# Attention and a low-rank mixed feed-forward block on one core: each raw weight block loaded as two transfers of half a row

## The chip, the cores and the metric

The kernel runs on one core of a Trainium2 chip. A core has four engines that compute (TensorE for matrix products, VectorE, ScalarE, GpSimd), SyncE, which here only issues transfers, and 16 DMA engines that move data between device memory (HBM) and on-chip memory. Each engine works through its own list of instructions in order; semaphores hold an instruction until what it needs is there. In the profile the engines are PE, DVE, ACT, POOL and SP. The metric is the device time of one execution in microseconds (us). One more execution of each kernel is recorded by the hardware profiler, and the rows below come from that one.

## The reference

The inputs are q, k and v (4 batches, 12 heads, 448 positions, 64 per head), two rank-32 matrices U and V, and two weight matrices w_ch1 (768 x 3072) and w_ch2 (3072 x 768). The scale is 1/8, the cap is 30.

```python
scores = scale * np.matmul(q, k.transpose(0, 1, 3, 2))
scores = cap * np.tanh(scores / cap)
scores = scores - np.max(scores, axis=-1, keepdims=True)
attn = np.exp(scores)
attn = attn / (np.sum(attn, axis=-1, keepdims=True) + 1e-09)
x = np.matmul(attn, v)              # heads put side by side: x is (4, 448, 768)
xt = x.transpose(0, 2, 1)
h = xt @ U @ V                      # mixing along the sequence
u = x + h.transpose(0, 2, 1)
ch = np.maximum(u @ w_ch1, 0.0) @ w_ch2
out = u + ch
```

The weights reach the kernel as raw words of 64 bits, so a block of 128 x 768 numbers is 128 rows of 6,144 bytes. The kernel turns them into 32-bit numbers itself.

## The kernel before

**Stages.** The program has three parts, which overlap at their edges. Up to about 225 us it is attention (scores, tanh, exp, product with v, the division by the sums, the mixing with U and V). From about 197 to 538 us comes the first pass of the feed-forward block, over batches 0 and 1; from 538 us on the second pass, over batches 2 and 3. A pass goes through the 24 blocks of 128 hidden columns in 12 chunks of two blocks. Products are kept at 32-bit accuracy by splitting each operand into a high and a low part, so one product is three matmuls.

**Up and down.** `up_seven` (matmuls of line 851) forms relu(u @ w_ch1) of one chunk by seven products of combined operands in place of eight plain ones. `down` (line 916) multiplies the result of one chunk by its two blocks of w_ch2, twelve products of six matmuls, and adds them to `u`. In the first pass the products of `down` for one chunk are laid between the products of `up_seven` for the next. The `down` of the last chunk has no next chunk in its pass: its 72 matmuls stand in one piece between the last product of the first pass and the first product of the second. In the second pass `down_seven` (line 1049) takes the place of `down`.

**Weights.** In the first pass `block` fetches a raw block into a buffer `wr` (two of them), `convert` makes 32-bit numbers of it in `wa`, and `keep` writes them to HBM, from where the second pass reads them. `convert` is three tasks: ScalarE takes the upper words (line 335), VectorE shifts the lower words (line 340), VectorE joins both (line 343). For w_ch2 `weights` then splits the block into its high part (ScalarE, line 284) and its low part (VectorE, line 754) in a buffer `w1`, which `down` multiplies by. The first of `down`'s six matmuls of a product use the chunk's first block, the other three its second block, so the second block of the last chunk, block 23 of w_ch2, is wanted from the fourth matmul of that `down` on.

**Operands of the second pass.** `operands` and `part` make the seven `x` buffers of a pass out of `u`: sums of two parts of `u` (VectorE, line 691, in a buffer that is also named `wr`), the high part (ScalarE or VectorE, lines 284 and 286) and the low part (VectorE, line 698). An `x` buffer of the second pass comes free when the first pass has done with it.

**What sets the order.** The order on every engine is fixed before the program runs. Each piece of work is a task with an assumed duration on the engines that can do it, a latency after which others may use its result, a priority (a lower number goes first) and the buffers that it needs. `simulate` runs through the tasks on a clock of its own: whenever an engine is free, it takes the ready task with the lowest priority number. The order that comes out is emitted. `rank` shifts the priorities between -150 and 0 by the table RANK. The chunks 10 and 11 of the first pass are prepared with -60, the operands of the second pass with -50; RANK adds 108 to the conversion, 56 to the operands and 6 to the splitting of w_ch2. So in the two last chunks a conversion has priority 48, an operand of the second pass 6, the splitting of w_ch2 -54, and the sums into `u` and the relu -200. A load is a task on SP with an assumed duration (350 for one transfer) and latency.

Of the kernel before, what the change touches and what calls it, by code (L numbers as in the profile page):

```python
# [14 lines left out]
I32 = mybir.dt.int32  # L15
# [4 lines left out]
DM = H * D  # L20
# [270 lines left out]
class Build(Plan):  # L291
# [417 lines left out]
    def block(self, which, f, first, begin, prio):  # L709

        nc = self.nc
        a = self.buf("wa", [128, DM], F32, self.wp, self.late)
        if not first:
            self.task({"SP": 350}, lambda: nc.sync.dma_start(out=a.t, in_=self.kept[which, f]),
                r=[("kept", which, f)], w=[(a, 0)], lat=4000, prio=prio)
            return a
        raw = self.buf("wr", [128, 2 * DM], I32, self.wq)

        def load():
            nc.sync.dma_start(out=raw.t, in_=self.w[which][f].bitcast(I32))  # L720

        def keep():
            d = self.kept[which, f] = self.dp.tile([128, DM], F32, tag="kept", name="kept", bufs=2 * NF)
            nc.scalar.dma_start(out=d, in_=a.t)

        self.task({"SP": 350}, load, w=[(raw, "u"), (raw, "l")], lat=7500, prio=prio, begin=begin)
        self.convert(raw, lambda: raw.t, a, lambda: a.t, prio, DM)
        self.task({"ACT": 120}, keep, r=[(a, 0)], w=[("kept", which, f)], lat=6500, prio=prio)
        return a
# [292 lines left out]
    def down_seven(self, order, bs, m, gq, vs):  # L1022
# [4 lines left out]
        u0, u1 = (self.u_bufs[b] for b in bs)  # L1027
        block = lambda u, d: ((lambda: u.t[:, d]), (u, d))
        onto = {3: lambda d: block(u1, d), 1: lambda d: block(u0, d), 6: lambda d: block(u0, 3 + d), 5: lambda d: block(vs, d),
            2: lambda d: block(u0, d), 7: lambda d: block(u1, 3 + d), 4: lambda d: block(u0, 3 + d)}  # L1030
        if final:
            at = range(order, order + 21)
# [4 lines left out]
        for n, (p, d) in enumerate((p, d) for p in porder for d in range(3)):  # L1037
            fresh = p not in (6, 5, 4)
            if fresh:
                bank[d] = self.bank()  # L1040
            ps = bank[d]

            def products(ps=ps, p=p, d=d, fresh=fresh):
                sl = slice(128 * d, 128 * d + 128)
                w, g = wo[p].t, [x.t for x in go[p]]
                n = 0
                for k in range(2):
                    for wi, gi in ((0, 0), (0, 1), (1, 0)):
                        nc.tensor.matmul(  # L1049
                            ps.t[:, :S], w[:, wi, k, sl], g[gi][:, k], start=fresh and n == 0, stop=n == 5,  # L1050
                            skip_group_check=not fresh)
                        n += 1

            self.task({"PE": 6 * 206}, products, r=[*((wo[p], i, k) for i in range(2) for k in range(2)), *((x, 0) for x in go[p])], w=[(ps, 0)],
                prio=next(at), mode="mm")
            out, key = onto[p](d)
            if p == 5 and m == 0:
                self.task({"ACT": 560}, lambda ps=ps, out=out: self.copy(nc.scalar, out(), ps.t[:, :S]), r=[(ps, 0)], w=[key],
                    prio=-200)
            elif p == 5 and final:  # L1060
                for x in (d, 3 + d):
                    self.onto(ps, *block(u1, x), False)
            else:
                self.onto(ps, out, key, n % 2 if not final else n < 15)
            yield
# [97 lines left out]
```

## Time and profile before

| what | value |
|---|---|
| median of 3 runs | 855.48 us (855.27 to 856.4) |
| profiled execution, its own time | 853.6 us |
| its span, first to last instruction | 851.8 us |
| matmuls busy (PE) | 840.4 us, 99% of the span |
| VectorE busy (DVE) | 691.0 us, 81% |
| ScalarE busy (ACT) | 527.6 us, 62% |
| moved by DMA | 136.51 MB, mean 160 GB/s |

The profiled execution's own time is 1.8 us more than its span. Busy time counts instructions that compute; issuing a transfer is not counted. A row of a waiting list says who waited for whom. A row of a timeline is one instruction, or several alike with their count (x3); in square brackets stands how long the engine was idle before it and what ended that.

### The profile page before, as it was taken

The page shows a single profiled execution, that of the slowest core. Times are in us where ns is not written, and L with a number is a line of the kernel's source. Part 1 is how long each engine was busy: PE and PEld are TensorE (multiplying, and loading weights), DVE is VectorE, ACT ScalarE, POOL GpSimd, SP SyncE. Part 2 cuts the span into 40 slices and gives each one's busy share as a digit, 9 for nine tenths or more (in the row PEclk, how much of TensorE's full clock was granted, in tenths as well). Part 3 has the DMA queues.
Part 4 walks back from the last instruction along what each step waited for, and adds up shares of the span by engine and source line. Part 5 has one row for each costly group of instructions (what it writes and reads, how often), then busy time and mean ns, then how long its engine had stood idle before and what let it go on. Part 6 is the DMA issues. An engine that isn't in the chain of part 4 may idle for free. (4 is left out here: it accounts for less than half of the span.)

```text
span 851.8 us, 11737 instructions
## 1 busy us (share of the span) xinstructions
PE 840.4 (99%) x4264; PEld 671.4 (79%) x4264; DVE 691.0 (81%) x1144; ACT 527.6 (62%) x789; POOL 146.1 (17%) x188
## 2 busy tenths in 40 slices
PE   9999999998999999999999999999999999999998
PEld 5334334346899999999999899999999999999997
DVE  2799889999887777877778699789888788888786
ACT  7999899885555355545555465456655555656472
POOL 0111111111022122122122122102111111111142
PEclk9999999999999999999999999999999999999999
DMA  6752443423578878787877866714427354262479
GB/s 225 241 172 84 160 148 96 146 68 93 183 190 259 245 188 249 191 265 211 231 231 207 252 162 151 215 48 120 114 36 179 68 143 93 53 170 42 122 136 224
DMA packets 51354, 136.51 MB, mean 160 GB/s; under 512 B 6720, under 2 KB 27104, under 8 KB 51296
## 3 DMA queue, kind: packets, MB, share of 16 engines
q1 hardware_dynamic: 23024, 79.29, 28.3%
q0 software_dynamic: 21360, 37.59, 24.6%
q10 hardware_dynamic: 6912, 18.88, 5.7%
q8 instruction: 33, 0.54, 0.3%
q14 instruction: 25, 0.20, 0.1%
HBM read 79.28 MB, written 24.47 MB: 122 GB/s over the span
## 5 line engine op out<-in xcount | busy, mean ns | idle before, releaser
L851 PE MATMUL mm<-x,ws 128*128 128x448 f32 x1512 | 332.7, 367 | 1.4 <-ACT cx L284 0.8
L851 PEld LDWEIGHTS mm<-x,ws 128*128 128x128 f32 x1512 | 283.3, 188 | 27.3 <-ACT cx L284 1.2
L916 PE MATMUL mm<-g,w 128*128 128x448 f32 x864 | 187.0, 366 | 0.6 <-DVE cx L864 0.3
L916 PEld LDWEIGHTS mm<-g,w 128*128 128x128 f32 x864 | 162.0, 188 | 15.0 <-ACT st L284 0.9
L1049 PE MATMUL mm<-g,w 128*128 128x448 f32 x696 | 154.9, 366 | 0.0
L284 ACT ACTIVATE st<-mm 128x448 f32<-128x448 f32 x133 | 72.4, 544 | 113.7 <-PE mm L916 55.2
L1049 PEld LDWEIGHTS mm<-g,w 128*128 128x128 f32 x696 | 130.6, 188 | 11.8
L929 POOL DMA_DIRECT2D u<-st x72 | 62.5, 868 | 268.9 <-ACT st L284 263.8
L1084 POOL DMA_DIRECT2D u<-st x57 | 49.4, 866 | 224.1 <-ACT st L284 161.4
L498 ACT ACTIVATE th<-sc,qsc 128x896 f32<-128x896 f32 x84 | 80.3, 1005 | 11.9 <-PE sc L493 11.7
L493 PE MATMUL sc<-qk 64*128 64x448 f32 (+1 forms) x384 | 77.8, 573 | 0.0
L508 ACT ACTIVATE th<-th,capt 128x1792 f32<-128x1792 f32 x42 | 75.2, 1790 | 0.8
L921 DVE TENSOR_TENSOR u<-u,mm 128x448 f32<-128x448 f32 x72 | 44.5, 618 | 21.6 <-PE mm L916 19.9
L534 PE MATMUL o<-th,vn 128*64 128x448 f32 x288 | 59.4, 548 | 0.0
L493 PEld LDWEIGHTS sc<-qk 64*128 64x128 f32 (+1 forms) x384 | 27.2, 175 | 37.2 <-issue 18.9
L343 DVE SCALAR_TENSOR_TENSOR wa<-wa,wr 128x768 int32<-128x768 int32 (+2 forms) x50 | 46.7, 935 | 11.1 <-ACT wa L335 10.3
L698 DVE TENSOR_TENSOR ws<-ta,ws 128x384 fp32r<-128x384 f32 x96 | 53.0, 552 | 3.2 <-ACT ws L284 2.9
L1079 DVE TENSOR_TENSOR u<-u,mm 128x448 f32<-128x448 f32 x57 | 35.0, 619 | 23.3 <-PE mm L1049 21.7
L540 DVE TENSOR_TENSOR es<-es,th 128x896 f32<-128x896 f32 (+1 forms) x44 | 47.5, 1082 | 6.0 <-ACT th L508 5.5
L335 ACT ACTIVATE wa<-wr 128x768 f32<-128x768 f32 (+2 forms) x50 | 44.1, 884 | 3.8 <-DVE wr L340 2.4
L534 PEld LDWEIGHTS o<-th,vn 128*64 128x64 f32 x288 | 18.5, 136 | 32.8 <-issue 30.0
L284 ACT ACTIVATE ws<-ta 128x384 fp32r<-128x384 f32 x64 | 32.9, 519 | 15.2 <-PE mm L851 8.9
(118 smaller groups left out, 957.5 us busy)
## 6 DMA issues: line engine op xcount, KB each, us to landing
wr<-in_w SPq DMA_DIRECT2D x48, 768.0 KB, 5.7
u<-st POOLq DMA_DIRECT2D x129, 224.0 KB, 4.1
kept<-wa ACTq DMA_DIRECT2D x48, 384.0 KB, 5.8
qk<-in_qk SPq DMA_DIRECT2D x24, 448.0 KB, 4.0
wr<-kept SPq DMA_DIRECT2D x24, 384.0 KB, 3.7
wa<-kept SPq DMA_DIRECT2D x24, 384.0 KB, 4.0
vn<-in_v SPq DMA_DIRECT2D x12, 448.0 KB, 3.7
rb<-rd POOLq DMA_DIRECT2D x24, 224.0 KB, 3.7
```

What stands on the lines that cost most here:

```text
L284: e.activation(out=out, in_=in_, func=func)
L493: nc.tensor.matmul(ps.t[out, a, :S], qks[c].t[hd, 1, 128 * t:min(S, 128 * t + 128)], qks[c].t[hd, 0], start=True, stop=True)
L498: nc.scalar.activation(out=th.t[:, j], in_=ps.t[:, :, :S], func=AF.Tanh, scale=self.qsc)
L508: nc.scalar.activation(out=th.t, in_=th.t, func=AF.Exp, scale=self.capt)
L534: nc.tensor.matmul(o.t[64 * a:64 * a + 64, :S], vn.t[:, 3 * i + t, a], th.t[:, j, a], start=False, stop=t == 2)
L540: e.tensor_tensor(out=out(), in0=in0(), in1=in1(), op=ALU.add)
L698: e.tensor_tensor(out=lo, in0=src(), in1=hi.bitcast(F32), op=ALU.subtract)
L851: nc.tensor.matmul(ps.t[:, :S], ws[p].t[:, wi, sl], xs[p].t[:, xi, d], start=fresh and n == 0, stop=n == 8, skip_group_check=not fresh)
L916: nc.tensor.matmul(ps.t[:, :S], w1[f].t[:, wi, sl], g[b, f].t[:, gi], start=f == fs[0] and i == 0, stop=f == fs[-1] and i == 2)
L929: nc.gpsimd.dma_start(out=u.t[:, d], in_=st.t, accum_op=ALU.add)
L1049: nc.tensor.matmul(ps.t[:, :S], w[:, wi, k, sl], g[gi][:, k], start=fresh and n == 0, stop=n == 5, skip_group_check=not fresh)
L1084: self.task({"POOL": 1000}, lambda: nc.gpsimd.dma_start(out=out(), in_=st.t, accum_op=ALU.add), r=[(st, 0)], w=[key], lat=6000, prio=-200)
```

## The change

The load of a raw block becomes two transfers, one for columns 0 to 767 and one for columns 768 to 1535 of its 1,536 words of 32 bits. Both go out on SP, one behind the other. The task's assumed duration on SP goes from 350 to 700 and its latency from 7500 to 7200.

```diff
         def load():
-            nc.sync.dma_start(out=raw.t, in_=self.w[which][f].bitcast(I32))
+            for i in range(2):
+                part = slice(DM * i, DM * i + DM)
+                nc.sync.dma_start(out=raw.t[:, part], in_=self.w[which][f].bitcast(I32)[:, part])
...
-        self.task({"SP": 350}, load, w=[(raw, "u"), (raw, "l")], lat=7500, prio=prio, begin=begin)
+        self.task({"SP": 700}, load, w=[(raw, "u"), (raw, "l")], lat=7200, prio=prio, begin=begin)
```

Since `simulate` reads both numbers, the order changes too. TensorE and GpSimd keep the order of their instructions from the first to the last. On VectorE and ScalarE the order is the same through attention and differs from the first pass on. Three places are shown. In the changed kernel, lines from 720 on have moved by up to 2, and the numbers behind the names differ between the two programs.

First place, VectorE in the last chunk of the first pass. Before, `wr_4344` is the raw block 23 of w_ch2 and `wa_4441` its converted form; `wr_4326` and `wa_4416` are block 22.

```order
L691 TENSOR_TENSOR ta_4346<-wa_4313,ta_4346 128x384
L340 TENSOR_SCALAR wr_4326<-wr_4326 128x768
L340 TENSOR_SCALAR wr_4344<-wr_4344 128x768
L864 TENSOR_TENSOR cx_4388<-cx_4388,mm_4240 128x448
L698 TENSOR_TENSOR ws_4427<-wa_4313,ws_4427 128x384
L921 TENSOR_TENSOR u1_558<-u1_558,mm_4420 128x448
L819 SCALAR_TENSOR_TENSOR g_4431<-cx_4388,g_4431 128x448
L343 SCALAR_TENSOR_TENSOR wa_4416<-wa_4416,wr_4326 128x768
L343 SCALAR_TENSOR_TENSOR wa_4441<-wa_4441,wr_4344 128x768
```

In the changed kernel block 22 is `wr_4405` and `wa_4518`, and block 23 is `wr_4431` and `wa_4548`.

```order
L691 TENSOR_TENSOR ta_4443<-wa_4408,ta_4443 128x384
L340 TENSOR_SCALAR wr_4405<-wr_4405 128x768
L286 CAST ws_4494<-wa_4408 128x384
L866 TENSOR_TENSOR cx_4299<-cx_4299,mm_4318 128x448
L698 TENSOR_TENSOR ws_4492<-ta_4443,ws_4492 128x384
L698 TENSOR_TENSOR ws_4494<-wa_4408,ws_4494 128x384
L821 SCALAR_TENSOR_TENSOR g_4507<-cx_4299,g_4507 128x448
L923 TENSOR_TENSOR u1_562<-u1_562,mm_4496 128x448
L698 TENSOR_TENSOR ws_4503<-ta_4447,ws_4503 128x384
L691 TENSOR_TENSOR ta_4443<-wa_4386,ta_4443 128x384
L343 SCALAR_TENSOR_TENSOR wa_4518<-wa_4518,wr_4405 128x768
```

Block 22 is converted at the same place as before; the two instructions for block 23 are no longer beside it.

Second place, VectorE from the relu of the last product of the first pass on (`g_4777` before; `mm_4549` is that product). `w1_4769` is the split form of block 23, and `mm_4782` the first product of the `down` that follows.

```order
L754 TENSOR_TENSOR w1_4769<-wa_4441,w1_4769 128x768
L819 SCALAR_TENSOR_TENSOR g_4777<-mm_4549,g_4777 128x448
L698 TENSOR_TENSOR ws_4779<-ta_4574,ws_4779 128x384
L698 TENSOR_TENSOR x_4702<-wr_4495,x_4702 128x448
L921 TENSOR_TENSOR u0_197<-u0_197,mm_4782 128x448
L691 TENSOR_TENSOR wr_4495<-u2_935,wr_4495 128x448 x3
L921 TENSOR_TENSOR u0_197<-u0_197,mm_4803 128x448
L698 TENSOR_TENSOR x_4813<-wr_4495,x_4813 128x448 x3
L921 TENSOR_TENSOR u0_197<-u0_197,mm_4829 128x448
L691 TENSOR_TENSOR wr_4495<-u2_935,u3_1355 128x448 x3
```

In the changed kernel the same relu is `g_4812<-mm_4581`, the split form of block 23 is `w1_4857`, and the first product of the `down` is `mm_4862`.

```order
L821 SCALAR_TENSOR_TENSOR g_4812<-mm_4581,g_4812 128x448
L698 TENSOR_TENSOR ws_4814<-ta_4679,ws_4814 128x384
L691 TENSOR_TENSOR wr_4593<-wr_4593,u2_939 128x448
L691 TENSOR_TENSOR wr_4593<-u2_939,wr_4593 128x448 x2
L698 TENSOR_TENSOR x_4769<-wr_4593,x_4769 128x448
L698 TENSOR_TENSOR x_4822<-wr_4593,x_4822 128x448 x2
L691 TENSOR_TENSOR wr_4593<-u2_939,wr_4593 128x448
L691 TENSOR_TENSOR wr_4593<-u2_939,u3_1360 128x448 x2
L698 TENSOR_TENSOR x_4822<-wr_4593,x_4822 128x448
L698 TENSOR_TENSOR x_4832<-wr_4593,x_4832 128x448
L691 TENSOR_TENSOR wr_4593<-u2_939,u3_1360 128x448
L698 TENSOR_TENSOR x_4832<-wr_4593,x_4832 128x448
```

The rows that come next there:

```order
L698 TENSOR_TENSOR x_4835<-u3_1360,x_4835 128x448
L698 TENSOR_TENSOR x_4832<-wr_4593,x_4832 128x448
L698 TENSOR_TENSOR x_4835<-u3_1360,x_4835 128x448 x2
L340 TENSOR_SCALAR wr_4431<-wr_4431 128x768
L343 SCALAR_TENSOR_TENSOR wa_4548<-wa_4548,wr_4431 128x768
L756 TENSOR_TENSOR w1_4857<-wa_4548,w1_4857 128x768
L964 TENSOR_TENSOR wr_4847<-wr_4847 128x2x384
L923 TENSOR_TENSOR u0_197<-u0_197,mm_4862 128x448
```

The conversion and the splitting of block 23 stand behind the last of the operands of the second pass, and the sums into `u` that stood between these operands stand behind it.

Third place, ScalarE behind the same relu. Before, the high part of block 23 (`w1_4769`) is the row ahead of it:

```order
L284 ACTIVATE w1_4769<-wa_4441 128x768
L284 ACTIVATE g_4777<-mm_4549 128x448
L284 ACTIVATE ws_4779<-ta_4574 128x384
L284 ACTIVATE st_4810<-mm_4793 128x448
L284 ACTIVATE x_4813<-wr_4495 128x448 x3
```

In the changed kernel:

```order
L284 ACTIVATE g_4812<-mm_4581 128x448
L284 ACTIVATE x_4769<-wr_4593 128x448
L284 ACTIVATE x_4822<-wr_4593 128x448 x3
L284 ACTIVATE x_4832<-wr_4593 128x448
L284 ACTIVATE x_4835<-u3_1360 128x448
L284 ACTIVATE x_4832<-wr_4593 128x448
L284 ACTIVATE x_4835<-u3_1360 128x448 x2
L284 ACTIVATE x_4832<-wr_4593 128x448
L726 DMA kept_4853<-wa_4548 128x768
L284 ACTIVATE w1_4857<-wa_4548 128x768
L284 ACTIVATE w1_4885<-wr_4855 128x768
L284 ACTIVATE st_4887<-mm_4869 128x448
```

Here too the high part of block 23 has moved behind the operands, and the store of the converted block is issued just ahead of it.

## Rows read from the trace of the kernel before

**Rows 1.** The page's first part: busy time, share of span, count.
```profile
PE   840.4 (99%) x4264; PEld 671.4 (79%) x4264; DVE 691.0 (81%) x1144; ACT 527.6 (62%) x789; POOL 146.1 (17%) x188
```

**Rows 2.** The waits of PE: total us, times, longest us.
```profile
PE misc L624 <- DVE u L602: 1.7, 1, 1.7
...
PE mm L916 <- DVE cx L864: 0.3, 1, 0.3
PE mm L916 <- ACT st L284: 0.2, 1, 0.2
```

**Rows 3.** Timeline of PE around the end of the first pass: start, us, instruction.
```profile
521.24 2.02 PE L851 MATMUL mm<-x,ws 128*128 128x448 f32 x9
523.10 14.73 PE L916 MATMUL mm<-g,w 128*128 128x448 f32 x72
537.68 7.59 PE L851 MATMUL mm<-x,ws 128*128 128x448 f32 x36
```

**Rows 4.** Timeline of DVE in the last chunk and behind the last product.
```profile
477.11 0.56 DVE L340 TENSOR_SCALAR wr<-wr 128x768 int32<-128x768 int32 x1
477.76 0.96 DVE L343 SCALAR_TENSOR_TENSOR wa<-wa,wr 128x768 int32<-128x768 int32 x1
...
487.10 0.56 DVE L340 TENSOR_SCALAR wr<-wr 128x768 int32<-128x768 int32 x1 [1.37 <-DMA wr<-in_w]
...
490.20 1.82 DVE L343 SCALAR_TENSOR_TENSOR wa<-wa,wr 128x768 int32<-128x768 int32 x2
...
522.82 0.96 DVE L754 TENSOR_TENSOR w<-wa,w 128x768 fp32r<-128x768 f32 x1
523.88 0.62 DVE L819 SCALAR_TENSOR_TENSOR g<-mm,g 128x448 fp32r<-128x448 f32 x1
524.42 0.55 DVE L698 TENSOR_TENSOR ws<-ta,ws 128x384 fp32r<-128x384 f32 x1
...
525.95 1.69 DVE L691 TENSOR_TENSOR wr<-u,wr 128x448 f32<-128x448 f32 x3
527.56 0.61 DVE L921 TENSOR_TENSOR u<-u,mm 128x448 f32<-128x448 f32 x1
```

**Rows 5.** Timeline of ACT (ACTq: its transfers) in the same stretch.
```profile
492.06 0.36 ACTq L724 DMA_DIRECT2D kept<-wa  x1
...
521.95 0.84 ACT L284 ACTIVATE w<-wa 128x768 fp32r<-128x768 f32 x1
523.30 0.54 ACT L284 ACTIVATE g<-mm 128x448 fp32r<-128x448 f32 x1 [0.52 <-PE mm L851]
```

**Rows 6.** The waits of SP's queue: total us, times, longest us.
```profile
SPq L720 <- DVE wa L343: 254.4, 45, 20.1
...
SPq L720 <- DMA wr<-in_w: 25.4, 15, 3.5
```

**Rows 7.** DMA issues between 220 and 500 us: count, KB each, us to landing.
```profile
wr<-in_w SPq DMA_DIRECT2D x40, 768.0 KB, 5.7
...
wr<-kept SPq DMA_DIRECT2D x2, 384.0 KB, 5.8
```

**Rows 8.** Timeline of SP's queue: two transfers issued behind one another.
```profile
492.06 0.84 SPq L949 DMA_DIRECT2D wr<-kept  x2
```

**Rows 9.** The waits of ACT on transfers that add into `u`.
```profile
ACT st L284 <- DMA u<-st: 18.5, 9, 4.0
```

**Rows 10.** Windows behind the last matmul: busy us by engine, granted clock (PEclk), DMA.
```profile
847.00:848.00 1.00, 0.67 (x4) 0.27 (x2) 0.40 (x2) 0.00 (x0) 0.00 (x0) 1.00 1.00 375
...
850.00:851.00 1.00, 0.00 (x0) 0.00 (x0) 0.00 (x0) 0.00 (x0) 0.00 (x0) 0.62 0.43 160
```

**Rows 11.** Timeline of PE at the start of the program.
```profile
1.21 3.57 PE L420 MATMUL misc<-ta 128*128 128x192 f32 x10 [1.21 <-POOL ta L417]
4.70 2.97 PE L493 MATMUL sc<-qk 64*128 64x448 f32 x8
...
9.99 2.22 PE L420 MATMUL misc<-ta 128*128 128x192 f32 x12
```

## The prediction

> **What bounds the kernel now.** I read the page's first part first: TensorE computes for 840.4 of 851.8 us [rows 1], so only 11.4 us of the span are without a matmul, some 4 of them behind the last one (it ends at 847.67) [rows 10]. The waits of PE come next: the longest is 1.7 us, in attention, and in the first pass line 916 waits 0.3 and 0.2 us [rows 2]. In the timeline of PE the first pass ends, the 72 matmuls of the last `down` run and the second pass begins without a gap [rows 3]. So there is almost nothing to win, and whatever makes TensorE wait once in the two passes is paid in full: no later gap is there to take it up. The question is thus only whether the change makes TensorE wait, and where.
>
> **The loads themselves.** 48 loads become 96 transfers. Each costs SP one more issue, 0.42 us as two in a row show [rows 8]; SP only issues transfers, and its queue waits 254.4 us for a raw buffer to be released by the conversion against 25.4 us for transfers [rows 6]. Loads are thus asked for as soon as a buffer is free, well ahead of use. Behind a load's second half in SP's queue stand further loads, for which the same holds. A whole block took 5.7 us to land [rows 7]; two halves are not in the trace. Bounds: a load of half the size took 5.8 us at the same time [rows 7], so a pair, whose second half is issued 0.42 us later, lands after 6.2 us, or after 11.6 us if the halves run one after the other. The nearest row is the whole block, since the bytes are the same, so I take 6.2 us, 0.5 us later. VectorE waited 1.37 us for a load once in the last chunk [rows 4], and TensorE ran on. Taken at nothing; bounds -0.5 us (both waits of line 916 gone [rows 2]) and +3 us (a few late loads that reach TensorE).
>
> A rule speaks to this. The rows show ScalarE waiting 18.5 us for transfers that add into `u` [rows 9], while loads are under way beside them. The Trainium skill, page "DMA: Bandwidth & Descriptors", section "Queues, rings and completion order", says that a DMA engine takes turns between queues packet by packet. By it shorter rows would let the adding transfers through sooner and the loads later. No row here shows the turns. By the rule the sum would lie up to 0.5 us lower, by the rows alone it stays.
>
> **The order.** The dear part is not the load but the plan made with its new numbers. TensorE keeps its order. On VectorE the conversion of block 23 of w_ch2 (lines 340 and 343) stood in the last chunk, and ran at 487.10 and, as second of two, from about 491.1 us [rows 4]. Its priority is 48, that of the second pass's operands 6. In the new plan it misses the place before the operands begin and comes behind all of them. The last 17 operand instructions of VectorE stand behind the relu of the first pass's last product, and this relu waits for that product. So the conversion cannot run while TensorE is still busy with the first pass, and the `down` that needs block 23 is next on TensorE.
>
> What that costs, step by step. The 72 matmuls run from 523.10 to 537.68, 0.2025 us each [rows 3]. The first three use block 22; the fourth and fifth need the high part of block 23, the sixth (at 523.10 + 5 x 0.2025 = 524.11) also its low part. VectorE's relu starts at 523.88 and the instruction on `ws` at 524.42 [rows 4]; both stand at the same place in the changed kernel, behind the same product, so these times hold. From there:
> - `ws`, 0.55 us [rows 4]: to 524.97.
> - 17 instructions on operands (7 sums of line 691, 10 low parts of line 698). Three of them took from 525.95 to 527.56, the start of the next, 0.537 us each [rows 4]: 9.12 us, to 534.09.
> - Line 340, whose join starts 0.65 us after it (477.11 to 477.76), and the join, line 343, 0.96 us [rows 4]: to 535.70.
> - On ScalarE the store of the block, which waits for the join and stands ahead of the high part: 0.36 us; the high part, 0.84 us [rows 5]: to 536.90.
> - The low part on VectorE, 0.96 us [rows 4]: to 537.86.
>
> The sixth matmul starts at 537.86 in place of 524.11: **13.75 us** later, in which TensorE does two matmuls. Beside the 9.12 us ScalarE makes ten high parts, some 0.55 us each by the like copy of the relu [rows 5], 5.5 us in all; if none of it were hidden the wait would be 5.5 us longer. The sums and low parts are interleaved three deep, as they were before, so I take none, and keep 2 us of it for the range. Could it be shorter? The 17 instructions follow one another in order, and nothing removes one. Without the store, 0.36 us less.
>
> What is behind the waiting instructions: on TensorE 67 matmuls of the `down` and the whole second pass, which shift as one. On VectorE the sums into `u` stand behind the low part and behind a combination of second-pass weights (line 964) that waits for a load into the buffer the operands have just left; that buffer is free at about 533, and such a load of 384 KB took 5.8 us in the busy stretch [rows 7], so it lands by 539, a microsecond after VectorE is ready. TensorE meanwhile fills other banks of PSUM at 1.2 us a product. Taken at nothing, up to 1.5 us if the banks run out.
>
> **The clock.** At the end of the program the granted clock is still 1.00 in the microsecond in which the last matmul ends (847.67), and between 850 and 851 the mean is 0.62: it fell from 2.4 to 1.2 GHz there [rows 10]. TensorE would wait from 523.7 to 536.9, four times as long as those 3 us, so I expect it to resume at 1.2 GHz. What that costs is bounded by the start of the program, the other place where TensorE comes out of idleness: the same matmul takes 0.357 us each from 1.21 on and 0.185 us from 9.99 on, and the eight of line 493 that end at 7.67 take 0.371 us each [rows 11]. At most 6.5 us ran at the lower level there, of which half would be lost, 3.2 us; at the least nothing. The row is the only one, but the matmuls there are few and come slowly, so I take 2.2 us.
>
> **The sum.** 13.75 + 2.2 = 16.0 us. On the profiled execution: 853.6 + 16.0 = 869.6 us. The median of the runs, 855.48, lies 1.9 us above the profiled execution; the shift is the same there: **871.5 us**, 1.9% slower.
>
> **Rivals.**
> - *The wait is there, the clock is not* (chance 0.17). TensorE does not slow, or is back at 2.4 GHz with the first matmuls. 855.48 + 13.75 = 869.2 us. For it: two matmuls run in the middle of the wait's end. Against it: the fall within 3 us [rows 10].
> - *The loads are late as well* (0.12). Where the queues are full, halves land by up to a second load later, VectorE and ScalarE wait for them in order, and sums behind them hold PSUM banks. For it: whole loads were already waited for [rows 4]. Against it: TensorE ran through these waits. 871.5 + 3 = 874.5 us.
> - *Not slower* (0.04). The shorter rows let the adding transfers pass, ScalarE's 18.5 us of waiting [rows 9] shrink, and the first pass's work on VectorE runs far enough ahead that block 23 is ready in time. The price would be -0.5 us at best, 855.0 us. It decides if the join of block 23 ends before 522.9 (the fourth matmul at 523.7 less 0.84 us for the high part), and the order forbids that: the join stands behind a relu that starts at 523.88.
> - The forecast holds the rest, 0.67. That the halves shorten the load and this pays is no case of its own: all waits of the two passes together are too small to see.
>
> **How the numbers follow.** The lower end: 13.75 less the store's 0.36, no clock, and the 1.9 us between median and profiled execution gone, gives 855.48 + 11.5 = 867. The upper end: 16.0 plus 2 for high parts that do not hide, 1 more for the clock (its bound of 3.2), 1.5 for the banks or half of the late loads, gives 855.48 + 20.5 = 876. Outside lie the last rival and the far end of the second. About 0.2%, 1.7 us, is what a measurement of this kernel can tell from no change. The first, second and main case are slower; the 0.04 of the last divide into 0.02 within 0.2% and 0.02 faster.
>
> **What would show it.** In the trace of the changed kernel: a gap on PE in line 918 of some 13 us, right behind the first three of 72 matmuls, put down to ScalarE or VectorE making `w`; on VectorE lines 340 and 343 as the last two instructions ahead of it, around 534 to 536 us; the second pass's first matmul (line 853) near 553 to 554 in place of 537.68; the granted clock at half for a few microseconds before or after the gap's end; in the second pass the same spacing as before. Wrong would be: no such gap; a gap below 10 us, which would mean that VectorE had done operands ahead of the relu; or gaps in the first pass, which would mean that the loads cost something by themselves.

## The result and the profile after

The changed kernel takes 867.88 us (median of 4 runs, 867.38 to 872.47) against 855.94 us (4 runs, 855.27 to 859.07) of the kernel before: 12 us slower, ratio 1.0146 with an interval of 1.011 to 1.0182. Its profiled execution took 872.47 us, the longest of the four. The forecast was 871.5 us with a range of 867 to 876: the sign, the place and the mechanism hold, the time lies 3.6 us under the forecast. Most of those 3.6 us go to a term that the forecast took at nothing, the loads themselves.

The first row that tells the story is in the waits of PE in the profile after (total us, times, longest us). Before, the longest wait was 1.7 us [rows 2]:

```profile
PE mm L918 <- ACT w L284: 13.0, 1, 13.0
PE misc L624 <- DVE u L602: 2.0, 1, 2.0
```

Where it stands is seen in PE's timeline after, around the end of the first pass (start, us, instruction, in brackets the idle time ahead of it):

```profile
524.58 1.99 PE L853 MATMUL mm<-x,ws 128*128 128x448 f32 x9
526.40 0.77 PE L918 MATMUL mm<-g,w 128*128 128x448 f32 x3
540.16 17.31 PE L918 MATMUL mm<-g,w 128*128 128x448 f32 x69 [12.99 <-ACT w L284]
557.30 3.00 PE L853 MATMUL mm<-x,ws 128*128 128x448 f32 x14
```

Before, 72 matmuls stood here in one piece and took 14.58 us from the first of them to the second pass [rows 3]. Now it is 557.30 - 526.40 = 30.90 us. Three matmuls run, 13 us pass without one, and the 69 others need 17.14 us where 69 x 0.2025 = 13.97 would do. So a gap is followed by a slow stretch.

VectorE's timeline after, from the relu of the last product on, answers to [rows 4]:

```profile
527.18 0.62 DVE L821 SCALAR_TENSOR_TENSOR g<-mm,g 128x448 fp32r<-128x448 f32 x1 [0.22 <-ACT g L284]
527.72 0.55 DVE L698 TENSOR_TENSOR ws<-ta,ws 128x384 fp32r<-128x384 f32 x1
528.19 0.62 DVE L691 TENSOR_TENSOR wr<-wr,u 128x448 f32<-128x448 f32 x1
528.72 1.15 DVE L691 TENSOR_TENSOR wr<-u,wr 128x448 f32<-128x448 f32 x2
529.79 1.69 DVE L698 TENSOR_TENSOR x<-wr,x 128x448 fp32r<-128x448 f32 x3
...
536.22 1.15 DVE L698 TENSOR_TENSOR x<-u,x 128x448 fp32r<-128x448 f32 x2
537.29 0.55 DVE L340 TENSOR_SCALAR wr<-wr 128x768 int32<-128x768 int32 x1
537.87 0.96 DVE L343 SCALAR_TENSOR_TENSOR wa<-wa,wr 128x768 int32<-128x768 int32 x1
540.14 0.96 DVE L756 TENSOR_TENSOR w<-wa,w 128x768 fp32r<-128x768 f32 x1 [1.31 <-ACT w L284]
541.01 0.95 DVE L964 TENSOR_TENSOR wr<-wr 128x768 f32<-128x768 f32 x1
...
545.18 0.96 DVE L971 TENSOR_TENSOR w<-wr,w 128x768 fp32r<-128x768 f32 x1 [2.63 <-ACT w L284]
```

VectorE works without a pause from 527.18 to 538.8: it is not idle, it does the operands of the second pass first. ScalarE's timeline after shows the last step of the chain (ACTq is its transfers); its first row is ScalarE taking the upper words of block 23:

```profile
498.56 0.90 ACT L335 ACTIVATE wa<-wr 128x768 f32<-128x768 f32 x1
...
538.86 0.35 ACTq L726 DMA_DIRECT2D kept<-wa  x1
539.26 0.84 ACT L284 ACTIVATE w<-wa 128x768 fp32r<-128x768 f32 x1 [3.77 <-DVE wa L343]
544.31 0.84 ACT L284 ACTIVATE w<-wr 128x768 fp32r<-128x768 f32 x1 [4.20 <-DMA wr<-kept]
```

The store goes out, the high part is made by 540.10, and TensorE resumes at 540.16. Block 23 itself was not late: ScalarE took its upper words at 498.56, 38.7 us before VectorE came to its lower words at 537.29. The granted clock in windows of the profile after (window, its length, busy us of PE, PEld, DVE, ACT and POOL, granted clock, share of the DMA engines, GB/s):

```profile
527.00:529.00 2.00, 0.17 (x1) 0.00 (x0) 1.82 (x4) 0.31 (x2) 0.00 (x0) 1.00 0.68 115
529.00:531.00 2.00, 0.00 (x0) 0.00 (x0) 2.00 (x5) 1.48 (x3) 0.00 (x0) 0.63 0.00 0
531.00:540.00 9.00, 0.00 (x0) 0.00 (x0) 7.80 (x14) 4.18 (x8) 0.00 (x0) 0.50 0.29 89
540.00:546.00 6.00, 5.84 (x15) 4.83 (x16) 3.23 (x4) 1.38 (x3) 0.07 (x1) 0.50 0.83 294
546.00:548.00 2.00, 2.00 (x10) 1.80 (x10) 0.76 (x2) 0.22 (x1) 0.79 (x1) 0.86 0.40 75
548.00:550.00 2.00, 2.00 (x11) 1.86 (x10) 0.62 (x1) 0.32 (x1) 0.87 (x1) 1.00 0.62 167
```

TensorE's last matmul ended at 527.17; the clock fell from 2.4 to 1.2 GHz between 529 and 531, was still there while the first 15 matmuls ran, and came back between 546 and 548. That is the slow stretch.

The loads themselves look harmless. DMA issues of the profile after between 220 and 500 us (count, KB each, us to landing), beside [rows 7]:

```profile
wr<-in_w SPq DMA_DIRECT2D x80, 384.0 KB, 5.3
kept<-wa ACTq DMA_DIRECT2D x41, 384.0 KB, 4.9
u<-st POOLq DMA_DIRECT2D x60, 224.0 KB, 4.9
```

A half lands after 5.3 us where a whole block took 5.7; both halves of a block have landed 6.1 us after the first was issued (median of the 40 pairs), close to the 6.2 that the forecast took. SP's queue still waits far longer for a raw buffer than for a transfer (beside [rows 6]):

```profile
SPq L722 <- DVE wa L343: 230.0, 41, 20.9
...
SPq L722 <- DMA wr<-in_w: 29.2, 19, 4.8
```

### The profile page after: what moved, and what is told of

Same layout as the page of the kernel before. It is cut to its first block, busy times and chain, and to the rows that moved or that the text cites. A ratio compares the mean times of both kernels' runs of the same rounds, so it can differ in the third digit from the quotient of the medians.

```text
span 870.7 us, 11868 instructions
## 1 busy us (share of the span) xinstructions
PE 845.6 (97%) x4264; PEld 675.4 (78%) x4264; DVE 693.7 (80%) x1151; ACT 527.2 (61%) x782; POOL 146.5 (17%) x188
## 3 DMA queue, kind: packets, MB, share of 16 engines
q1 hardware_dynamic: 29936, 79.30, 28.1%
## 4 chain that ended last, share of the span: by engine, by line
PE 88%; DVE 5%; ACT 3%; DMA 2%; issue 1%; POOL 0%; ACTq 0%; DVEq 0%; POOLq 0%
PE mm L853 35%; PE mm L918 21%; PE mm L1051 18%; PE o L534 5%; PE sc L493 5%; DMA rb<-rd 1%; PE misc L640 1%; ACT th L498 1%; ACT th L508 1%; DVE x L698 1%; PE misc L420 1%; DVE es L540 1%; PE o L522 1%; PE misc L624 1%; PE misc L573 1%
## 5 line engine op out<-in xcount | busy, mean ns | idle before, releaser
L343 DVE SCALAR_TENSOR_TENSOR wa<-wa,wr 128x768 int32<-128x768 int32 (+2 forms) x50 | 46.3, 934 | 8.7 <-ACT wa L335 8.1
L866 DVE TENSOR_TENSOR cx<-cx,mm 128x448 f32<-128x448 f32 x36 | 22.3, 619 | 30.8 <-PE mm L853 26.4
```

## The experiments

The theory: the loss is the order alone, made by the two assumed numbers; the halves cost nothing. Rivals: the halves are the loss, or part of it; or the clock is a part of it that can be bought back. "Before" is the kernel before, run beside them: 856.76 us (17 runs) beside the first four, 855.42 (17) beside the next four, 857.3 (11) beside the last four. The diffs are against the kernel after, unless they say otherwise.

**Halves without the new plan** (`e1_halves_old_plan`): two transfers, the old numbers, hence the order of before.

```diff
-        self.task({"SP": 700}, load, ..., lat=7200, prio=prio, begin=begin)
+        self.task({"SP": 350}, load, ..., lat=7500, prio=prio, begin=begin)
```

> The loads in two halves, but the task's assumed numbers as before (350 and 7500), so that every engine has the order of the kernel before. Theory P (the order alone costs): no gap ahead of the fourth matmul of the last down, ratio to before 0.998 to 1.002. Theory L (the halves themselves cost, by more rows and more issues): a part of the measured 12 us stays, ratio 1.004 or more, with new waits of TensorE spread over the first pass. A third possibility, that halves help by letting the transfers that add into u through sooner: ratio up to 0.999, as TensorE's waits in the first pass are 0.5 us in all.

Measured: 855.3 us (12 runs, 851.32 to 859.24), ratio 0.9982 (0.9959 to 1.0005). PE's timeline of this kernel has the 72 matmuls in one piece again:

```profile
526.60 14.73 PE L918 MATMUL mm<-g,w 128*128 128x448 f32 x72
541.17 24.12 PE L853 MATMUL mm<-x,ws 128*128 128x448 f32 x116
```

The halves cost nothing. If anything they win 1.5 us, which the interval of this run does not separate from zero.

**The new plan without halves** (`e2_whole_new_plan`): whole loads, the new numbers. The diff is against before.

```diff
-        self.task({"SP": 350}, load, ..., lat=7500, prio=prio, begin=begin)
+        self.task({"SP": 700}, load, ..., lat=7200, prio=prio, begin=begin)
```

> The loads whole, as before, but the task's assumed numbers as in the changed kernel (700 and 7200), so that every engine has the order of the changed kernel. Theory P: the gap of some 13 us ahead of the fourth matmul of the last down is there, and the time is that of the changed kernel, ratio to before 1.012 to 1.018. Theory L: clearly less, near 1.005 or below.

Measured: 872.87 us (6 runs, 870.52 to 874.32), ratio 1.0184 (1.0155 to 1.0214). PE's timeline:

```profile
525.07 0.77 PE L916 MATMUL mm<-g,w 128*128 128x448 f32 x3
538.83 16.94 PE L916 MATMUL mm<-g,w 128*128 128x448 f32 x69 [12.99 <-ACT w L284]
555.61 9.66 PE L851 MATMUL mm<-x,ws 128*128 128x448 f32 x46
```

The same gap, with every byte loaded as before: the order makes the loss, all of it. It makes even more than the whole loss, 16.1 us.

**The kernel after, beside them** (`after_again`).

> The changed kernel once more, beside the others. Both theories: ratio 1.012 to 1.018. Its trace is a second look at the gap: 13 us wherever the run as a whole stands, with TensorE at half clock behind it for 3 to 6 us.

Measured: 868.84 us (6 runs, 867.64 to 871.78), ratio 1.0146 (1.0116 to 1.0177), 4 us under the whole loads with the same order. That was a new question; the last runs return to it.

**TensorE kept busy in the gap** (`e4_after_fill`): 58 matmuls into a bank that the first product then overwrites, ahead of the last `down`.

```diff
-                def products(ps=ps, sl=sl, b=b):
+                def products(ps=ps, sl=sl, b=b, k=k):
+                    for _ in range(58 if fs[-1] == NF - 1 and not k else 0):
+                        nc.tensor.matmul(
+                            ps.t[:, :S], w1[fs[0]].t[:, 0, sl], g[b, fs[0]].t[:, 0], start=True, stop=True)
```

> The changed kernel with 58 matmuls more, whose result is overwritten, ahead of the first product of the last down: 58 x 0.2025 = 11.7 us of work inside the gap. If the clock is a part of the price (2.2 us by the forecast, about 3 us in the trace of the changed kernel), the granted clock stays at 1.00, the 69 matmuls behind the wait take 14.0 us, and the time falls by 2 to 3 us against the changed kernel, ratio 1.010 to 1.014 to before. If the clock costs nothing, or is back at once, the time is that of the changed kernel. If the wait were shorter than 12 us, the filling would make it slower.

Measured: 869.88 us (6 runs, 867.69 to 871.25), ratio 1.0153 (1.0121 to 1.0185): no gain. PE's timeline and two windows of this kernel:

```profile
524.01 11.99 PE L917 MATMUL mm<-g,w 128*128 128x448 f32 x58
535.84 0.77 PE L921 MATMUL mm<-g,w 128*128 128x448 f32 x3
537.77 0.67 PE L921 MATMUL mm<-g,w 128*128 128x448 f32 x2 [1.16 <-ACT w L284]
538.77 4.11 PE L921 MATMUL mm<-g,w 128*128 128x448 f32 x19 [0.32 <-DVE w L756]
543.35 9.99 PE L921 MATMUL mm<-g,w 128*128 128x448 f32 x48 [0.48 <-ACT st L284]
553.18 12.12 PE L853 MATMUL mm<-x,ws 128*128 128x448 f32 x59
```

```profile
524.00:536.00 12.00, 12.00 (x60) 11.04 (x59) 11.74 (x23) 5.65 (x11) 0.22 (x1) 1.00 0.19 39
536.00:553.00 17.00, 15.04 (x73) 12.96 (x72) 6.78 (x10) 4.19 (x7) 4.35 (x5) 1.00 0.90 254
```

The clock stayed at 2.4 GHz throughout, and block 23 came as late as ever: 537.77 - 524.01 = 13.76 us, as in the kernel after. From there to the second pass it took 15.41 us in place of 17.14, not 13.97: at the full clock TensorE waited for the low part (0.32 us) and for a bank (0.48 us). These two waits are 0.8 of the 1.44 us over 13.97. So in the trace the clock is worth 1.7 us net against that execution, 1.3 against the second trace of the kernel after and 0.3 against the third, and the medians don't show it, although the recorded mean clock of all six executions is 0.997 to 1.000 (0.988 to 0.991 for the kernel after beside them). I had expected more; this is a miss.

**The block moved forward by one priority** (`e5_after_convert65`).

```diff
-    ("convert", 108),
+    ("convert", 65),
```

> The kernel after with one number of RANK changed: the conversion gets 65 in place of 108 added to its priority. The loads stay two halves with the assumed 700 and 7200, so the first pass is still planned from the new numbers, but in the plan the conversion and the split of block 23 of w_ch2 stand ahead of the operands of the second pass again. Theory P (the loss is the place of block 23 in the order, nothing else): no gap in line 918, 14.6 us from the first matmul of the last down to the first of the second pass, as before, and 853 to 857 us, ratio 0.995 to 1.001 to the kernel before. Theory N (numbers 700 and 7200 spoil the order in other places too, or the halves cost something under this plan): no gap there, but 858 us or more, with new waits of TensorE elsewhere in the first pass. If the halves save something by themselves, as the runs so far hint (1.5 us under the old order, 4 us under the new one), the time lies in the lower half of the range, under 855.

Measured: 854.01 us (12 runs, 851.16 to 858.29), ratio 0.9977 (0.9952 to 1.0001). VectorE's timeline of this kernel holds the conversion of the last block over 20 us ahead of the transition and its split just ahead of the last relu; PE's has no gap:

```profile
498.47 0.56 DVE L340 TENSOR_SCALAR wr<-wr 128x768 int32<-128x768 int32 x1
...
499.47 0.95 DVE L343 SCALAR_TENSOR_TENSOR wa<-wa,wr 128x768 int32<-128x768 int32 x1
...
521.36 0.96 DVE L756 TENSOR_TENSOR w<-wa,w 128x768 fp32r<-128x768 f32 x1 [0.36 <-ACT w L284]
```

```profile
521.62 14.76 PE L918 MATMUL mm<-g,w 128*128 128x448 f32 x72
536.22 24.07 PE L853 MATMUL mm<-x,ws 128*128 128x448 f32 x118
```

The change's halves and numbers remain, one priority differs, and the loss is gone. It is the lowest median of all kernels, but its interval ends at 1.0001: better than after, and by this run alone not shown better than before.

**Only the assumed latency, and the other way** (`e6_whole_lat7550`): the kernel before with 50 more.

```diff
-        self.task({"SP": 350}, load, ..., lat=7500, prio=prio, begin=begin)
+        self.task({"SP": 350}, load, ..., lat=7550, prio=prio, begin=begin)
```

> The kernel before with the assumed latency of a load changed from 7500 to 7550 and nothing else: whole loads, 350 on SP. The plan that comes out has block 23 of w_ch2 behind all 17 operand instructions of the second pass and one more instruction of ws behind the relu. Theory P: the same gap as after, 13 us plus 0.3 to 0.55 for the one more instruction, so 13.3 to 13.6 us idle on PE in line 916, and 869 to 874 us, ratio 1.014 to 1.021, though not a byte is loaded otherwise. Rival H (halves are needed for the loss, because a load that lands late is what holds the conversion back): no gap or a small one, 855 to 859 us.

Measured: 872.38 us (4 runs, 870.59 to 875.18), ratio 1.0193 (1.0167 to 1.0219). PE's timeline:

```profile
526.86 0.77 PE L916 MATMUL mm<-g,w 128*128 128x448 f32 x3
541.25 16.10 PE L916 MATMUL mm<-g,w 128*128 128x448 f32 x69 [13.62 <-ACT w L284]
557.19 3.00 PE L851 MATMUL mm<-x,ws 128*128 128x448 f32 x14
```

For the loss, neither a second transfer nor a second issue is needed. A change of 0.7% in one assumed number drops the conversion behind the operands. The gap is 0.63 us longer; 0.3 to 0.55 was expected for the one more instruction.

**Where the halves win: early blocks only** (`e8_first_half_halves`).

```diff
-            for i in range(2):
-                part = slice(DM * i, DM * i + DM)
+            for i in range(2 if f < 12 else 1):
+                part = slice(DM * i, DM * i + DM) if f < 12 else slice(0, 2 * DM)
```

> The kernel after, with the blocks of both weights up to number 11 loaded as halves and the later twelve of each as whole rows; the plan and the order are those of the kernel after. The gap of 13 us must be there in any case. The question is where the halves win the 4 us that lie between the medians of the kernel after (868.8) and of whole loads under the same order (872.9). If they win it in the early part, where attention and the first chunks share the queues: 868 to 870 us. If they win it late in the first pass: 871.5 to 874 us. If the 4 us was only scatter between the runs: the same time as the whole loads of the next run, within 1.5 us.

Measured: 871.63 us (6 runs: 867.37, 867.95, 871.56, 871.7, 873.35, 875.63), ratio 1.0177 (1.0147 to 1.0208). The median lies in the range named for whole loads, the single runs on both sides of it; this does not decide the question.

**Whole loads once more** (`e2_whole_again`).

> Whole loads under the order of the kernel after, once more: a second measure of what halves do under the same order. It was 872.87 us (870.52 to 874.32) beside 868.84 for the kernel after. If halves win something themselves: again 871.5 to 874 us, ratio 1.016 to 1.021. If that was scatter: 868 to 871 us, ratio 1.012 to 1.016.

Measured: 872.39 us (6 runs, 871.16 to 877.1), ratio 1.0199 (1.0172 to 1.0227), as the first time.

**Four kernels of one order side by side.** The kernel after (`after_third`):

> The kernel after once more, beside whole loads, quarters and half of the blocks in halves, all four with the same order of instructions. Theory H (halves win about 4 us by themselves under this order): 867 to 869.5 us, 3 to 4.5 us under the whole loads of the last of these runs. Theory S (the 4 us between medians is scatter between the runs): within 1.5 us of the whole loads. In either case the gap of 13.0 us in line 918 and 16 us from the first matmul of the last down to the second pass on top of the 14.6 of before.

Measured: 868.78 us (5 runs, 867.02 to 871.21), ratio 1.0144 (1.0118 to 1.017). Whole loads (`e2_whole_third`):

> Whole loads under the order of the kernel after, for the comparison with the three others beside it: 871.5 to 874 us, ratio 1.016 to 1.021, as twice before.

Measured: 872.18 us (5 runs, 869.78 to 873.5), ratio 1.0171 (1.0148 to 1.0194). Both sets together, the kernel after has 11 runs with mean 869.2 us, whole loads 17 with mean 872.5: 3.3 us apart, with 1.3 us as twice the standard error (3.1 us if the set of whole loads that had no kernel after beside it is left out). So the 4 us were not scatter alone. Nor is it the clock alone: among the executions with a recorded mean clock of 0.989 to 0.991, the kernel after has 8 with mean 868.9 us, whole loads 11 with mean 871.9. Halves of the later blocks only (`e10_second_half_halves`, the diff of the early blocks with `f >= 12`):

> The kernel after with only the blocks from number 12 on of both weights loaded as halves; the loads that run beside attention are whole. The order is that of the kernel after. If the halves win their 4 us in attention (the first matmul of the first pass lay between 195.7 and 200.9 us in the traces so far, and this is where traces differ): 871.5 to 874 us, as for whole loads. If they win it in the second half of the first pass: 867 to 869.5 us.

Measured: 871.79 us (4 runs, 870.6 to 872.71), ratio 1.017 (1.0146 to 1.0194), as for whole loads. So the late blocks alone don't bring it. Quarters (`e9_quarters_new_plan`):

```diff
-            for i in range(2):
-                part = slice(DM * i, DM * i + DM)
+            for i in range(4):
+                part = slice(DM // 2 * i, DM // 2 * i + DM // 2)
```

> The kernel after, but each raw block goes out as four transfers of a quarter row (1,536 bytes); the assumed numbers and so the order stay. Theory H (shorter rows help the other transfers): at or below the kernel after, 865 to 868.5 us. Rival I (what the halves win is lost again to the issues on SP, four times 0.42 us each block, or to smaller packets): 870 to 875 us. Theory S (scatter): equal to the kernel after and to whole loads within 1.5 us.

Measured: 870.64 us (6 runs, 868.33 to 875.73), ratio 1.0166 (1.0138 to 1.0193): no better than halves, between them and whole loads. That is in the range of rival I, but by the means it lies 2.4 us over the kernel after with 2.6 us as twice the standard error, so it is not separated from it.

## Why the prediction was right, and where it was not

**The order: right, in its steps.** Ten traces have the gap. In nine of them the fourth matmul of the last `down` starts 13.76 us after the first (541.25 - 526.86 = 14.39 in the tenth, with one instruction more). The forecast put the high part at 536.90, 13.80 us after the first matmul. Step by step in the profile after: the 17 operands took 537.29 - 528.19 = 9.10 us (9.12); L340 to L343 0.58 (0.65); L343 to the end of the high part 540.10 - 537.87 = 2.23 (2.16). ScalarE's high parts were all hidden. TensorE would have done its fourth matmul after 0.61 us, so the shift is 13.15 us; the forecast's 13.75 counted to the sixth matmul, which needs the low part. Counted in that way it holds too: in the profile after the low part ends at 541.10 and the sixth matmul starts 14.75 us after the first, where the forecast has 537.86 - 523.10 = 14.76. That the plan and not a load is the cause is shown by four kernels that agree: whole loads have the gap with the new numbers, and with 50 more of latency; halves lose it with the old numbers, and with another priority for the conversion.

**The clock: right in size, and not all of it to be had.** 2.2 us were forecast. The 69 matmuls took 15.65 to 17.14 us up to the second pass in the ten traces, 2.4 us over 13.97 in the mean, 1.7 to 3.2 in single ones, all within the bounds of 0 to 3.2. The excess is half of the time that passed at 1.2 GHz after TensorE resumed: 6.4 us and 3.17 in the profile after, 3.2 us and 1.71 in the third trace of that kernel (windows above and at the end). In one of the ten traces (halves in the early blocks) 0.3 us of it is the sixth matmul's wait for the low part. With the clock held up by the fill, 1.44 us over 13.97 remained, 0.8 of it the two waits. The rival without the clock (869.2 us) lies nearer to the measured median than the forecast, but for another reason: the clock did fall in the trace of the kernel after. That the median lies inside the range is in part luck: its lower end of 867 was made by taking away the clock and the 1.9 us between median and profiled execution, and what pulled the time down was something else.

**The sum of both** is 13.15 + 2.4 = 15.55 us in the traces (forecast 16.0). Whole loads in the new order, which have this and nothing else, measured 16.1, 17.0 and 14.9 us over before, 16.0 in the mean.

**The step that failed is "The loads themselves"**, taken at nothing with bounds of -0.5 and +3 us. Under the new order the halves win 3.3 us, more than the lower bound allows, and this puts the kernel at 868 to 869 and not at 872. I had bounded the gain by the two waits of line 916 [rows 2], as if only the passes could gain; but a trace of one execution holds little of what varies between executions. Under the good order both kernels with halves are lower too (1.5 and 1.4 us), each time within its interval of nothing; taken together as above, their 24 runs have mean 854.4 us and the 34 of before beside them 856.3, 2.0 us apart with 1.3 as twice the standard error. So halves seem to win some 2 to 3 us with the gap and without it. Where the gain lies is not settled. It is not in the transition: there 30.9, 30.4 and 29.4 us for halves stand against 30.5, 30.8 and 29.4 for whole loads. The late blocks alone don't bring it, and traces of one kernel differ most ahead of the first pass: in the three of the kernel after its first matmul starts between 195.97 and 199.51 us (195.69 to 200.92 in all traces), while the first pass up to the last `down` takes 325.7 to 327.8 us. That points to the loads beside attention, but the kernel with halves in the early blocks alone did not confirm it.

What the halves do to other transfers is seen in the waits of ScalarE. In the profile after (answering to [rows 9]), and below it in the first kernel with whole loads and the same order:

```profile
ACT st L284 <- DMA u<-st: 6.1, 3, 2.5
```

```profile
ACT st L284 <- DMA u<-st: 13.1, 6, 3.1
```

Three traces of each lie at 6.0 to 8.0 and at 12.4 to 13.5 us. The Trainium skill, page "DMA: Bandwidth & Descriptors", section "Queues, rings and completion order", says that a DMA engine takes turns between queues packet by packet. By that rule, smaller packets would let others through sooner, and with halves the traces agree: the adding transfers land after 4.8 to 4.9 us beside halves and 5.2 to 5.4 beside whole loads. With quarters they agree only in part: the stores of the converted blocks land after 4.1 us (4.7 to 4.9 beside halves, 6.0 to 6.2 beside whole loads), but the adding transfers after 5.6. The packets did get smaller: SP's queue moved its 79.3 MB in 23,024 packets before, 29,936 after and 43,760 with quarters. No run shows the turns themselves. The waits for adding transfers are ScalarE's, and TensorE did not wait behind them.

**The load behind the low part** was in time. Line 964 starts at 541.01, right behind the low part and without a wait; its two transfers, issued at 536.32 and 536.70, had landed by 540.30. What the forecast did not have is the second such buffer, which ScalarE takes next: its transfers went out at 538.86 and 539.22, and ScalarE waited for them until 544.31. No wait of TensorE followed it in that trace, in which TensorE ran at 1.2 GHz meanwhile; in the kernel with the fill, at 2.4 GHz, ScalarE waited likewise until 542.02, its copies out of PSUM stood behind that, and TensorE waited 0.48 us for a bank. The forecast had such waits for banks at nothing, 1.5 us at most.

## What to carry to other kernels

Where a planner orders the instructions, an edit of its assumed numbers can change the order of every engine's work, as it did here on two engines: compare the order ahead of the time, and look on each engine for work that has slid behind something that can't start early. Split such a change into its transfers and its numbers and time both alone; here one wins 3.3 us and the other loses 16. On an engine that is 99% busy, as TensorE here, the gap cost its full length, and 1.7 to 3.2 us more behind it while the clock was down.

## What the runs showed of the hardware

- The clock's return after the same gap differs between executions of the same kernel. In the profile after it was at half up to 546, six us after TensorE resumed. In the third trace of that kernel, where TensorE resumed at 535.44, these windows have it back after some 3 us:

```profile
535.00:538.00 3.00, 2.56 (x6) 1.94 (x7) 2.42 (x3) 0.39 (x1) 0.00 (x0) 0.50 0.94 305
538.00:541.00 3.00, 3.00 (x15) 2.75 (x15) 0.54 (x1) 1.28 (x2) 0.00 (x0) 0.89 0.87 291
541.00:543.00 2.00, 2.00 (x11) 1.87 (x10) 1.13 (x3) 0.54 (x1) 1.35 (x2) 1.00 0.29 65
```

- The stretch of 40 to 60 us in attention ran at a granted clock of 1.00 in some executions and below in others. The lowest is in the kernel with halves in the early blocks alone:

```profile
40.00:60.00 20.00, 17.55 (x84) 6.66 (x80) 13.92 (x23) 14.80 (x16) 2.35 (x4) 0.83 0.52 160
```

Its first pass also began latest of all, at 200.92 us; the kernel with the other priority, at 1.00 there, began it at 195.69. The clock of this stretch is not all: halves with the old numbers, at 1.00 there too, began it at 199.02. In nine of the fourteen traces the clock was also at 0.96 in the mean from 195 to 240 us (the profile after is one), in the other five at 1.00 (the kernel before, the third trace of the kernel after). A scatter of 851 to 863 us in kernels without the gap fits this, and the recorded mean clock goes with it (1.000 in the execution of before at 852.13 us, 0.991 in the one at 863.33), but the clock of those other executions stretch by stretch was not seen.
